# An attention loop with its steps reordered, its keys and queries split once per head pair, and a shorter weight conversion

## The chip, the cores and the metric

The kernel runs on one core of a Trainium2 chip. The metric is the device time of one execution in microseconds. Engines are named as the profile names them: PE (matrix multiply), PEld (its weight loads), DVE (vector), ACT (scalar), POOL (GpSimd) and SP (the queue from which nearly all DMAs of the attention stage are issued).

## What is computed

Attention over 4 batches and 8 heads, with queries averaged in pairs, then a switch layer with 8 experts, then a product layer. Cut to what matters:

```python
q_pool = q.reshape(B, H, S // 2, 2, D).mean(axis=3)      # B, H, S, D = 4, 8, 1152, 64
scores = np.matmul(q_pool, k.transpose(0, 1, 3, 2)) / np.sqrt(D)
attn = softmax(scores)
x = np.matmul(attn, v)                                   # 2304 tokens of 512
# tokens with x @ w_skip > 0 go through one expert: relu(xc @ w1[e]) @ w2[e]
# then h = (x @ m1) * (x @ m2); out = (h @ w3) @ w_out
```

Everything is held to float32 accuracy, so an operand is split into a rounded high part and a low remainder where the matmul runs in the faster `float32r` format.

## The kernel before

The attention stage walks 16 head pairs (4 batches times 4 pairs), nine steps a pair, 144 steps in one loop (L707). A step handles one tile of 128 queries of one head, or (the fifth of a pair, `TILES[l] is None`) the last 64 queries of both heads. In step `i` the program issues, for three different tiles at once:

- `emit_t(i-2)` and `emit_c`: nine 128 x 128 transposes of the exponentials of two steps earlier (L275), and their copies out of PSUM in three groups, by ACT, DVE and ACT (L294);
- `emit_e(i-1)`: the exponential of the step before, on ACT (L264), which needs the maximum;
- `emit_s(i)`: the score matmuls (L241), six of 384 columns, nine in the fifth step, into the same three PSUM banks that the transposes of this step used, each bank once its copy is done; then `emit_x(i)`, the row maximum on DVE (L252);
- two calls of `emit_pv`: each is one block of value matmuls (L311), two float32 matmuls of 64 weight columns, which the profile shows as four. A pair has 18 blocks, nine for its first 320 queries and nine for the other 256. This text calls such a block a value unit.

The order on PE is: value unit, transposes, value unit, scores. Each engine works through its own instructions in the order of the program. `tc.manual_schedule()` keeps the written order; waits between engines are semaphores that the framework sets from the data.

**Preparation.** While pair `p` runs, `prep(p+1, j)` at steps 1 to 6 makes the next pair's operands on POOL. The scores are exact because `KS[i][h]` holds the high part of a head's keys in partitions 0 to 63 and the low part in 64 to 127, and `QS[i][h][0]` holds the high part of the queries twice. So `load` fetches every head's keys and queries twice, into both halves of the partitions (eight DMAs of 64 partitions a pair), `prep_k` copies 128 partitions (L181) and subtracts in the upper 64 (L182), `prep_s` adds the two query halves and scales (L193, L194), `prep_q` splits (L203, L204) and fills `BD` (L206, 64 partitions). `ld_kh` copies the high keys of both heads into `KH` by two DMAs. All of it is done per head, with two buffers `i = p % 2`.

**Conversion.** Four weight matrices arrive as float64 and are turned into float32 in 40 chunks of 128 x 512 by `conv_ops`: three DVE operations on integers (L90, L93, L95) assemble the float's bits, POOL squares the high word (L91), and a fourth DVE operation (L97) sets tiny values to zero by that square. The result is stored by SP. `side` advances the conversion by two of its four parts a step (each `yield` ends a part) where no routing is under way.

**Routing.** After each batch of four pairs `route_ops` computes the expert of each token, in parts that `side` hands out; among them are POOL's ten indirect DMAs (L397, L410), which scatter token numbers, and five groups of output transposes (L430). In batches 0 to 2 these stand inside the loop: the scatters are issued in step 1 of pairs 6, 10 and 14, ahead of `prep(p+1, 0)`.

After the loop come the expert tiles and the output layer, from about 612 us on.

Of the kernel before, what the change touches and what calls it, by code (L numbers as in the profile page):

```python
# [43 lines left out]
def body(ctx, tc, q, k, v, w9, w1, w2, m1, m2, w3t, wo, cst, mcst, ids, out, dbg=None):  # L44
# [29 lines left out]
    def conv_ops(erl):  # L74
        def ld(name, c):
            h = erl.tile([128, CW, 2], I32, tag="ch", name="ch", bufs=3)
            SP.dma_start(h, wsrc[name].rearrange("(p n) t -> p n t", p=128)[:, c * CW:(c + 1) * CW, :])
            return h
        nxt = [ld(*conv_q[0]), ld(*conv_q[1])]
        yield  # L80
        st = None
        for n, (name, c) in enumerate(conv_q):
# [4 lines left out]
            m = erl.tile([128, CW], F32, tag="cm", name="cm", bufs=2)  # L87
            o = erl.tile([128, CW], F32, tag="co", name="co", bufs=2)
# [13 lines left out]
        SP.dma_start(*st)  # L102
# [13 lines left out]
    if True:  # L116
# [7 lines left out]
        KH = mid.tile([128, S], F32R, name="kh")  # L124
# [8 lines left out]
        def load(p, h):  # L133
            if p >= NP:
                return
            b, hp = divmod(p, NHP)
            r = slice(64 * h, 64 * h + 64)
            qr = erl.tile([128, 2, SQ], F32, tag="qr", name="qr", bufs=3)
            kr = erl.tile([128, S], F32, tag="kr", name="kr", bufs=3)
# [4 lines left out]
            rawq[p, h], rawk[p, h] = qr, kr  # L144

        def load_first():
            r = [slice(64 * h, 64 * h + 64) for h in range(2)]
            for h in range(2):
                rawq[0, h] = erl.tile([128, 2, SQ], F32, tag="qr", name="qr", bufs=3)
# [18 lines left out]
        def load_v(p):  # L168
# [3 lines left out]
            vr = mid.tile([128, 2, KT, HD], F32, tag="vr", name="vr", bufs=3)  # L172
# [14 lines left out]
        def prep_s(p, h, fast, c0=0, c1=SQ):  # L187
            qr = rawq[p, h]
            if c0 == 0:
                pre[p, h] = erl.tile([128, SQ], F32, tag="qsum", name="qsum", bufs=2)  # L190
# [19 lines left out]
        def ld_kh(p):  # L210
            if p < NP:
                for h in range(2):
                    SP.dma_start(f(KH[64 * h:64 * h + 64]), f(KS[p % 2][h][0:64]))

        def prep(p, j):
            if p >= NP:
                return
            h, u = divmod(j, 3)
            if u == 0:
                prep_k(p, h, 0, S, False)  # L220
            elif u == 1:
                prep_s(p, h, False)
            else:
                prep_q(p, h, False)
# [5 lines left out]
        def emit_s(i, c, evac):  # L230
# [4 lines left out]
            if t is None:  # L235
                seq = [(qs[h][0][:, 512:640], ks[h]) for h in range(2)] + [(BD[p % 2], KH)]
# [206 lines left out]
        def side(kinds):  # L443
# [239 lines left out]
        with tc.manual_schedule():  # L683
# [18 lines left out]
            ld_kh(0)  # L702
            for h in range(2):
                load(1, h)
            load_v(1)
            SP.dma_start(tab.rearrange("(p n) o -> p (n o)", p=128), padt)
            for i in range(NSTEP + 7):  # L707
# [8 lines left out]
                if l in (4, 7):  # L716
                    load(p + 2, l // 7)
                if l == 0 and p >= 1:
# [5 lines left out]
                for n in (2 * i - 14, 2 * i - 13):  # L724
# [7 lines left out]
                if pvs[0]:  # L732
                    emit_pv(*pvs[0])
# [9 lines left out]
                if pvs[1]:  # L743
# [214 lines left out]
```

## Time and profile before

| what | us |
|---|---|
| median of three runs | 1169.83 |
| lowest and highest run | 1162.92, 1172.56 |
| span of the profiled execution | 1168.7 |
| of that, attention stage | 0 to 612 |

The page and the rows below come from one profiled execution; the record gives its span, from the first instruction to the last, and no separate total for it. All stretches of time are counted from the start of that span. A busy PE is not PE at its peak, since matmuls are pipelined and their ends are modelled; so the distance between the starts of two runs of matmuls is used here, not their busy time. In the timeline equal instructions in a row stand on one line with their count, and a bracket gives the idle time before and what ended it.

### The profile page before, as it was taken

The numbers are of one execution on the slowest core, as the hardware profiler recorded it, in microseconds if no ns is written. First come the engines' busy times: TensorE is split into PE (matmuls) and PEld (weight loads), VectorE is DVE, ScalarE is ACT, GpSimd is POOL, SyncE is SP. The second block draws the span as 40 slices with busy tenths as digits, with TensorE's granted clock in tenths as the row PEclk, the third lists the DMA queues.
The fourth block names the chain that finished last, engine by engine and source line by source line (L and its number), as shares of the span: only waits on it lengthen the run. The fifth ranks groups of instructions, "written<-read, shape, count | busy, mean of one in ns | idle before, by whom it ended". The sixth has DMA issues, their size and how long they took to land. (4 is left out here: it accounts for less than half of the span.)

```text
span 1168.7 us, 16655 instructions
## 1 busy us (share of the span) xinstructions
PE 1079.3 (92%) x6060; PEld 817.8 (70%) x6060; DVE 630.2 (54%) x880; ACT 474.9 (41%) x900; POOL 516.6 (44%) x473
## 2 busy tenths in 40 slices
PE   5999999997989978999999769999699999999995
PEld 4665665664556645656667658878498989999894
DVE  6699997666986659975653342425651212112120
ACT  3655554553546535555563042324442212212120
POOL 4975666049772378661693361445712020101100
PEclk9999998998999999999999979999899999999998
DMA  9867766367665287543351883243301010101000
GB/s 217 235 189 203 211 173 162 81 106 188 199 174 154 23 195 217 163 117 82 72 153 37 143 273 112 64 164 119 122 28 47 8 55 1 55 19 38 27 1 28
DMA packets 63881, 136.04 MB, mean 116 GB/s; under 512 B 13216, under 2 KB 22944, under 8 KB 63778
## 3 DMA queue, kind: packets, MB, share of 16 engines
q1 hardware_dynamic: 54578, 118.94, 38.8%
q0 software_dynamic: 6080, 14.26, 3.8%
q10 hardware_dynamic: 3120, 1.57, 0.7%
q8 instruction: 52, 0.85, 0.3%
q14 instruction: 51, 0.42, 0.1%
HBM read 103.93 MB, written 22.96 MB: 109 GB/s over the span
## 5 line engine op out<-in xcount | busy, mean ns | idle before, releaser
L252 DVE TENSOR_REDUCE sm<-s 128x1 f32<-128x1152 f32 x144 | 195.0, 1354 | 106.1 <-PE s L241 99.9
L241 PE MATMUL s<-k,q 128*128 128x384 f32 x864 | 208.2, 367 | 47.4 <-DVE pt L294 34.4
L241 PEld LDWEIGHTS s<-k,q 128*128 128x128 f32 x864 | 147.6, 193 | 117.3 <-ACT pt L294 46.3
L294 ACT COPY pt<-s 128x384 f32<-128x384 f32 x288 | 137.8, 479 | 211.6 <-PE s L275 210.3
L311 PE MATMUL vb<-pt,vr 128*64 128x256 f32 (+1 forms) x1152 | 204.8, 438 | 0.0
L275 PEld LDWEIGHTS s<-cs,p 128*128 128x128 f32 x1296 | 145.3, 145 | 68.4 <-issue 53.8
L264 ACT ACTIVATE p<-s,sm 128x1152 f32<-128x1152 f32 x144 | 177.0, 1229 | 38.9 <-DVE sm L252 38.9
L275 PE MATMUL s<-cs,p 128*128 128x128 f32 x1296 | 180.0, 286 | 2.0 <-ACT p L264 2.0
L883 POOL DMA_INDIRECT out_dram<-ar,ord x18 | 17.9, 993 | 272.8 <-ACT ar L882 268.1
L868 DVE TENSOR_TENSOR ar<-b,ar 128x384 f32<-128x384 f32 x48 | 26.8, 558 | 193.6 <-PE b L864 193.6
L311 PEld LDWEIGHTS vb<-pt,vr 128*64 128x64 f32 x1152 | 58.8, 137 | 60.6 <-issue 57.1
L182 POOL TENSOR_TENSOR k<-kr,k 64x1152 fp32r<-64x1152 f32 x31 | 83.4, 2689 | 33.8 <-DMA perm<-idt,sp 31.4
L294 DVE COPY pt<-s 128x384 f32<-128x384 f32 x144 | 79.5, 552 | 15.1 <-PE s L275 12.1
L869 ACT CAST CVh<-ar 128x384 fp32r<-128x384 f32 x48 | 24.7, 514 | 108.5 <-DVE ar L868 108.5
L397 POOL DMA_INDIRECT tab<-idt,si x20 | 19.9, 993 | 108.6 <-DVE sp L407 102.6
L91 POOL TENSOR_TENSOR cm<-ch 128x512 f32<-128x512 f32 x40 | 43.1, 1079 | 53.4 <-DVE co L97 36.7
L93 DVE SCALAR_TENSOR_TENSOR ca<-ch,ca 128x512 int32<-128x512 int32 x40 | 61.9, 1547 | 1.1
L497 PE MATMUL b<-W2h,CVh 128*128 128x512 f32 x176 | 60.7, 405 | 0.2
L497 PE MATMUL b<-W1h,CVh 128*128 128x512 f32 x176 | 60.1, 402 | 0.8 <-issue 0.7
L497 PE MATMUL b<-WPh,CVh 128*128 128x512 f32 x144 | 57.5, 399 | 0.0
L497 PE MATMUL b<-WPl,CVh 128*128 128x512 f32 x144 | 56.9, 395 | 0.0
L497 PE MATMUL b<-WPh,CVl 128*128 128x512 f32 x144 | 56.8, 395 | 0.0
(189 smaller groups left out, 1880.3 us busy)
## 6 DMA issues: line engine op xcount, KB each, us to landing
kr<-in_k_dram SPq DMA_DIRECT2D x62, 288.0 KB, 6.5
qr<-in_q_dram SPq DMA_DIRECT2D x60, 288.0 KB, 5.7
R<-in_w_dram SPq DMA_DIRECT2D x16, 1024.0 KB, 5.4
vr<-in_v_dram SPq DMA_DIRECT2D x16, 576.0 KB, 8.1
kh<-k SPq DMA_DIRECT2D x32, 288.0 KB, 4.7
ch<-in_w3t_dram SPq DMA_DIRECT2D x16, 512.0 KB, 4.1
ch<-in_m_dram SPq DMA_DIRECT2D x16, 512.0 KB, 4.2
x_d<-xr SPq DMA_DIRECT2D x16, 258.0 KB, 14.1
```

Source lines behind the costliest of these rows:

```text
L91: POOL.tensor_tensor(m, hf, hf, op=ALU.mult)
L93: DVE.scalar_tensor_tensor(a, h[:, :, 1], -0x40000000, a, op0=ALU.bitwise_and, op1=ALU.bitwise_or)
L182: (DVE if fast else POOL).tensor_tensor(ks[64:128, c0:c1], kr[64:128, c0:c1], f(ks[64:128, c0:c1]), op=ALU.subtract)
L241: m = PE.matmul(sp[:, c, 0:384], lhsT=lt, rhs=kk[:, 384 * c:384 * c + 384], start=(n == 0), stop=(n == len(seq) - 1))
L252: DVE.tensor_reduce(sm, sp[:, :, 0:384], axis=AX.XY, op=ALU.max, negate=True)
L264: ACT.activation(pt, sp[:, :, 0:384], AF.Exp, bias=sm, scale=1.0, accum_out=SM[b][:, hp, c:c + 1])
L275: m = PE.transpose(tp[:, u * 128:u * 128 + 128], src[:, kt * 128:kt * 128 + 128], ident)
L294: m = (DVE.tensor_copy(o, i_) if eng is DVE else ACT.copy(o, i_)).ins
L311: PE.matmul(acc[64 * h:64 * h + 64, 0:n], lhsT=vr[:, h, kt, :], rhs=pt[:, kt, h, :], start=(kt == 0), stop=(kt == KT - 1))
L497: PE.matmul(o, lhsT=lh[a], rhs=rh[b_], start=(first and n == 0), stop=(last and n == len(order) - 1))
L868: DVE.tensor_tensor(cv, pb[:, 0:GT], av, op=ALU.mult)
L869: ACT.copy(CV[0][:, c], cv)
```

## The change

The value units of a step move behind the exponential and stand together, ahead of the scores; they are issued half a step earlier in the loop's count. `load` fetches each pair's keys and queries once, in 128 partitions; POOL splits them once for both heads, in four preparation steps, and DMAs on SP stack the halves into `KS` and `QS`. `KH` is now where the split writes and has two buffers, so `ld_kh` remains for the first pair only. In the conversion the last DVE operation goes; POOL compares the square and multiplies (`mask`), one chunk later. The first two DVE operations now stand in one part, so a chunk has two parts, and `side` advances one part a step. Buffers of `qr`, `vr` and `qsum` drop from 3, 3, 2 to 2, 2, 1, those of `cm` rise to 3; the values are loaded at step 7.

```diff
+        def mask(name, c, a, m):
+            POOL.tensor_scalar(m, m, TINY * TINY, 1.0, op0=ALU.is_ge, op1=ALU.mult)
+            POOL.tensor_tensor(m, a.bitcast(F32), m, op=ALU.mult)
+            SP.dma_start(wd[name].rearrange("(p n) -> p n", p=128)[:, c * CW:(c + 1) * CW], m)
...
             DVE.tensor_scalar(a, h[:, :, 1], 0x07FFFFFF, 3, op0=ALU.bitwise_and, op1=ALU.logical_shift_left)
+            DVE.scalar_tensor_tensor(a, h[:, :, 1], -0x40000000, a, op0=ALU.bitwise_and, op1=ALU.bitwise_or)
             POOL.tensor_tensor(m, hf, hf, op=ALU.mult)
-            yield
-            DVE.scalar_tensor_tensor(a, h[:, :, 1], -0x40000000, a, op0=ALU.bitwise_and, op1=ALU.bitwise_or)
+            if st:
+                mask(*st)
+            st = (name, c, a, m)
             yield
             DVE.scalar_tensor_tensor(a, h[:, :, 0], 29, a, op0=ALU.logical_shift_right, op1=ALU.bitwise_or)
             yield
-            DVE.scalar_tensor_tensor(o, m, TINY * TINY, a.bitcast(F32), op0=ALU.is_ge, op1=ALU.mult)
-            if st:
-                SP.dma_start(*st)
-            st = (wd[name].rearrange("(p n) -> p n", p=128)[:, c * CW:(c + 1) * CW], o)
-            yield
...
-        def load(p, h):
+        def load(p):
...
-            for u in range(2):
-                SP.dma_start(qr[64 * u:64 * u + 64], q[b, hp, r])
-            for u in range(2):
-                SP.dma_start(kr[64 * u:64 * u + 64], k[b, hp, r])
+            SP.dma_start(rawk[p], k[b, hp])
+            SP.dma_start(rawq[p], q[b, hp])
...
         def prep(p, j):
...
+            if j == 0:
+                for c in range(3):
+                    cc = slice(384 * c, 384 * c + 384)
+                    POOL.tensor_scalar(kh[:, cc], rawk[p][:, cc], 1.0, 0.0, op0=ALU.mult, op1=ALU.add)
+                    POOL.tensor_tensor(KL[:, cc], rawk[p][:, cc], f(kh[:, cc]), op=ALU.subtract)
+                del rawk[p]
+            elif j == 1:
+                qr = rawq.pop(p)
+                s = pre[p] = erl.tile([128, SQ], F32, tag="qsum", name="qsum", bufs=1)
+                POOL.tensor_tensor(s, qr[:, 0], qr[:, 1], op=ALU.add)
+                POOL.tensor_scalar(s, s, 0.0625, 0.0, op0=ALU.mult, op1=ALU.add)
+            elif j == 2:
+                for h in range(2):
+                    r = slice(64 * h, 64 * h + 64)
+                    SP.dma_start(f(KS[i][h][0:64]), f(kh[r]))
+                    SP.dma_start(f(KS[i][h][64:128]), f(KL[r]))
+                s = pre.pop(p)
+                POOL.tensor_scalar(QN[0], s, 1.0, 0.0, op0=ALU.mult, op1=ALU.add)
+                POOL.tensor_tensor(QN[1], s, f(QN[0]), op=ALU.subtract)
+                for h in range(2):
+                    r = slice(64 * h, 64 * h + 64)
+                    POOL.tensor_scalar(BD[i][r, r], f(QN[1][r, 512:576]), 1.0, 0.0, op0=ALU.mult, op1=ALU.add)
             else:
-                prep_q(p, h, False)
+                for h in range(2):
+                    r = slice(64 * h, 64 * h + 64)
+                    for u in range(2):
+                        d = slice(64 * u, 64 * u + 64)
+                        if h == 0:
+                            SP.dma_start(f(QS[i][h][0][d, 0:576]), f(QN[0][r]))
+                        else:
+                            SP.dma_start(f(QS[i][h][0][d, 0:512]), f(QN[0][r, 0:512]))
+                            SP.dma_start(f(QS[i][h][0][d, 576:640]), f(QN[0][r, 512:576]))
+                        SP.dma_start(f(QS[i][h][1][d]), f(QN[1][r]))
...
-                if k is None:
-                    next(conv, None)
...
-                if l in (4, 7):
-                    load(p + 2, l // 7)
-                if l == 0 and p >= 1:
+                if l == 4:
+                    load(p + 2)
+                if l == 7 and p >= 1:
                     load_v(p + 1)
...
-                for n in (2 * i - 14, 2 * i - 13):
+                for n in (2 * i - 13, 2 * i - 12):
...
-                if pvs[0]:
-                    emit_pv(*pvs[0])
...
-                if pvs[1]:
-                    emit_pv(*pvs[1])
+                for u in pvs:
+                    if u:
+                        emit_pv(*u)
...
-                if ss and l == 6:
-                    ld_kh(p + 1)
-                if ss and 1 <= l <= 6:
+                if ss and 1 <= l <= 4:
                     prep(p + 1, l - 1)
```

## Rows read from the trace of the kernel before

**Rows 1.** Busy us of PE, PEld, DVE, ACT, POOL by stretch; clock, DMA share, GB/s

```profile
60.00:180.00 120.00, 115.16 (x712) 73.61 (x713) 113.64 (x123) 69.42 (x132) 80.08 (x72) 1.00 0.72 198
41.00:612.00 571.00, 534.66 (x3295) 345.39 (x3296) 439.36 (x553) 309.18 (x596) 350.50 (x317) 0.97 0.60 153
612.00:1168.70 556.70, 516.15 (x2633) 450.98 (x2633) 166.35 (x290) 146.32 (x271) 141.26 (x126) 0.97 0.24 70
```

**Rows 2.** Timeline of one clean step: start us, us, engine, line, operation [idle before]

```profile
588.43 1.32 PE L241 MATMUL s<-k,q 128*128 128x384 f32 x6
...
589.68 0.65 PE L311 MATMUL vb<-pt,vr 128*64 128x256 f32 x4
...
589.84 1.36 DVE L252 TENSOR_REDUCE sm<-s 128x1 f32<-128x1152 f32 x1 [1.66 <-PE s L241]
...
590.26 1.20 PE L275 MATMUL s<-cs,p 128*128 128x128 f32 x9
...
591.18 0.56 DVE L294 COPY pt<-s 128x384 f32<-128x384 f32 x1
...
591.40 0.65 PE L311 MATMUL vb<-pt,vr 128*64 128x256 f32 x4
...
591.88 1.23 ACT L264 ACTIVATE p<-s,sm 128x1152 f32<-128x1152 f32 x1
```

**Rows 3.** Score matmuls (L241) by stretch, one head pair each: PE, PEld, clock, DMA

```profile
76.60:111.30 34.70, 12.74 (x60) 9.52 (x58) 1.00 0.69 184
258.40:309.50 51.10, 14.59 (x58) 9.59 (x58) 0.90 0.75 204
418.80:468.10 49.30, 14.50 (x60) 9.87 (x58) 0.93 0.76 205
```

**Rows 4.** Timeline around the scatters of the second batch, POOL, DVE and PE

```profile
391.37 1.01 POOL L397 DMA_INDIRECT tab<-idt,si  x1 [34.03 <-DVE sp L407]
...
404.56 1.15 POOL L181 TENSOR_SCALAR k<-kr 128x1152 fp32r<-128x1152 f32 x1
...
416.43 2.65 POOL L182 TENSOR_TENSOR k<-kr,k 64x1152 fp32r<-64x1152 f32 x1 [10.72 <-DMA perm<-idt,sp]
...
431.44 1.09 DVE L97 SCALAR_TENSOR_TENSOR co<-cm,ca 128x512 f32<-128x512 f32 x1 [9.31 <-POOL cm L91]
...
434.98 1.65 PE L241 MATMUL s<-k,q 128*128 128x384 f32 x4 [6.39 <-DVE pt L294]
```

**Rows 5.** Timeline, DVE and POOL, at one preparation step

```profile
109.88 2.90 POOL L182 TENSOR_TENSOR k<-kr,k 64x1152 fp32r<-64x1152 f32 x1
...
110.31 3.03 DVE L93 SCALAR_TENSOR_TENSOR ca<-ch,ca 128x512 int32<-128x512 int32 x1
```

**Rows 6.** Groups of instructions, 41 to 612 us: count, busy us, mean ns, idle before

```profile
L97 DVE SCALAR_TENSOR_TENSOR co<-cm,ca 128x512 f32<-128x512 f32 x40 | 35.2, 879 | 22.3 <-POOL cm L91 19.3
...
L182 POOL TENSOR_TENSOR k<-kr,k 64x1152 fp32r<-64x1152 f32 x28 | 75.4, 2694 | 33.5 <-DMA perm<-idt,sp 31.4
...
L204 POOL TENSOR_TENSOR q<-qsum,q 128x512 fp32r<-128x512 f32 (+2 forms) x44 | 46.4, 1055 | 3.7
L193 POOL TENSOR_TENSOR qsum<-qr 128x576 f32<-128x576 f32 x28 | 45.1, 1610 | 1.6
L91 POOL TENSOR_TENSOR cm<-ch 128x512 f32<-128x512 f32 x40 | 43.1, 1079 | 53.4 <-DVE co L97 36.7 <-issue 11.1 <-DMA qr<-in_q_dram 4.2
```

**Rows 7.** Timeline of PE where runs stand beside other neighbours

```profile
564.85 1.32 PE L241 MATMUL s<-k,q 128*128 128x384 f32 x6
566.00 0.60 PE L430 MATMUL vb<-cs,ar 128*128 128x128 f32 x4
...
570.08 0.76 PE L311 MATMUL vb<-pt,vr 128*64 128x320 f32 x4
...
613.73 1.30 PE L311 MATMUL vb<-pt,vr 128*64 128x320 f32 x8
```

**Rows 8.** DMA issues: count, KB each, median us to landing

```profile
kh<-k SPq DMA_DIRECT2D x32, 288.0 KB, 4.7
```

More of the change, by code (lines that the diff above doesn't have):

```diff
@@ L123, in body @@
         BD = [mid.tile([128, 128], F32R, name=f"bd{i}") for i in range(2)]
-        KH = mid.tile([128, S], F32R, name="kh")
+        KH = [pl[i].tile([128, S], F32R, name=f"kh{i}") for i in range(2)]
+        KL = mid.tile([128, S], F32R, name="kl")
+        QN = [mid.tile([128, SQ], F32R, name=f"qn{x}") for x in "hl"]
         KS = [[pl[i].tile([128, S], F32R, name=f"k{h}{i}") for h in range(2)] for i in range(2)]
@@ L136, in load @@
             b, hp = divmod(p, NHP)
[L137 to L144 removed]
+            rawq[p] = erl.tile([128, 2, SQ], F32, tag="qr", name="qr", bufs=2)
+            rawk[p] = erl.tile([128, S], F32, tag="kr", name="kr", bufs=3)
+            SP.dma_start(rawk[p], k[b, hp])
+            SP.dma_start(rawq[p], q[b, hp])
         def load_first():
@@ L148, in load_first @@
             for h in range(2):
-                rawq[0, h] = erl.tile([128, 2, SQ], F32, tag="qr", name="qr", bufs=3)
+                rawq[0, h] = erl.tile([128, 2, SQ], F32, tag="qr", name="qr", bufs=2)
                 rawk[0, h] = erl.tile([128, S], F32, tag="kr", name="kr", bufs=3)
@@ L171, in load_v @@
             b, hp = divmod(p, NHP)
-            vr = mid.tile([128, 2, KT, HD], F32, tag="vr", name="vr", bufs=3)
+            vr = mid.tile([128, 2, KT, HD], F32, tag="vr", name="vr", bufs=2)
             SP.dma_start(vr, v[b, 2 * hp:2 * hp + 2].rearrange("h (p t) d -> p h t d", p=128))
@@ L189, in prep_s @@
             if c0 == 0:
-                pre[p, h] = erl.tile([128, SQ], F32, tag="qsum", name="qsum", bufs=2)
+                pre[p, h] = erl.tile([128, SQ], F32, tag="qsum", name="qsum", bufs=1)
             s = pre[p, h][:, c0:c1]
@@ L208, in prep_q, with ld_kh @@
                 del pre[p, h]
[L210 to L213, printed above, removed]
+        def ld_kh():
+            for h in range(2):
+                SP.dma_start(f(KH[0][64 * h:64 * h + 64]), f(KS[0][h][0:64]))
         def prep(p, j):
@@ L217, in prep @@
                 return
[L218 to L222, printed above, removed]
-            else:
-                prep_q(p, h, False)
+            i = p % 2
+            kh = KH[i]
+            if j == 0:
[20 more added lines that the diff above has]
+                    POOL.tensor_scalar(BD[i][r, r], f(QN[1][r, 512:576]), 1.0, 0.0, op0=ALU.mult, op1=ALU.add)
+            else:
+                for h in range(2):
+                    r = slice(64 * h, 64 * h + 64)
[7 more added lines that the diff above has]
+                        SP.dma_start(f(QS[i][h][1][d]), f(QN[1][r]))
         NSTEP = NP * NT9
@@ L235, in emit_s @@
             if t is None:
-                seq = [(qs[h][0][:, 512:640], ks[h]) for h in range(2)] + [(BD[p % 2], KH)]
+                seq = [(qs[h][0][:, 512:640], ks[h]) for h in range(2)] + [(BD[p % 2], KH[p % 2])]
             else:
@@ L701, in body @@
             prep_k(0, 1, 0, S, False)
-            ld_kh(0)
-            for h in range(2):
-                load(1, h)
+            ld_kh()
             load_v(1)
             SP.dma_start(tab.rearrange("(p n) o -> p (n o)", p=128), padt)
+            load(1)
             for i in range(NSTEP + 7):
```

5 lines of the change are left out of this document (2 added, 3 removed).

## The prediction

> **What bounds the kernel now.** I read the busy time by stage first. The attention stage (41 to 612 us) keeps PE busy for 534.7 of 571.0 us; after 612 us the program is the expert and output stage, which the change does not touch, so its 556.7 us are taken as they are [rows 1]. Inside attention I then read one clean step line by line [rows 2]: a score run starts at 588.43, the first value unit at 589.68, nine transposes at 590.26, the second value unit at 591.40. With the second unit as long as the first, the step is 1.25 + 0.58 + 1.14 + 0.58 = 3.55 us and PE never stops in it, so PE's own order sets its length. Steps whose value unit is 320 columns wide are 0.2 us longer, the ninth step of a pair has three more score matmuls (0.5 us); a pair of nine clean steps comes to 4 × 3.76 + 3.65 + 3 × 3.55 + 4.07 = 33.4 us, sixteen pairs to 534.6. The stage ends at 612, so 77 us are lost. 7.6 go to the start (the first pair takes 41 us) and about 16 to the routing matmuls of three batches, which PE must do anyway. The other 53 are stalls, and the pair windows show them [rows 3]: pair 2 takes 34.7 us, pairs 7 and 11 take 51.1 and 49.3. With 2.5 us of output transposes in each, these two lose 15 and 13, together 28; the remaining 25 are spread over the pairs in which weight conversion runs.
>
> Two causes stand behind the stalls. In pairs 7 and 11 POOL issues ten scatters of 1.0 us from 391.37 on and then sits until 416.43 for them to land; DVE, in order, waits 9.31 us for POOL's square (L91) before its last conversion step, and PE 6.39 us behind DVE's copy [rows 4]. In the conversion pairs DVE is busy 113.6 of 120 us [rows 1], and its conversion operations are long because they meet POOL: an L93 of 3.03 us at 110.31 stands beside a POOL subtraction of 2.90 us that began at 109.88 [rows 5], while L97, which seldom meets one, averages 0.88 [rows 6].
>
> **The change part by part.** *Order of the step.* Before, PE changes four times a step between 128-column and 64-column weights: scores, value unit, transposes, value unit, scores. After, it is scores, transposes, two value units, scores: two changes. What one change costs: two value units of 320 columns in a row last 1.30 us where one lasts 0.76 [rows 7], so the second adds 0.54; a separate one takes 0.58 plus the 0.11 by which 0.76 exceeds the narrow unit's 0.65 [rows 2], 0.69. The difference is 0.15. The other end: scores followed directly by 128-column transposes take 1.15 (564.85 to 566.00) instead of 1.25 [rows 7], and the transposes then start without the slower first one, which I put at 0.05. Sum 0.30 a step. Bounds: 0.25 if the transposes gain nothing, 0.33 if they gain 0.08. 137 steps have scores or transposes beside value units, so 137 × 0.30 = 41 us.
>
> What takes the place of the value unit ahead of the transposes? They need the exponential of two steps earlier. Counted from the start of the transposes of one step: the maximum starts 0.27 after it (the last score matmul drains, then 0.1), takes 1.36, the exponential 1.23 after that [rows 2], and about 0.15 passes until PE may go: 3.0 us. The new step is 3.55 - 0.30 = 3.25. So the wait is hidden by 0.2 us in a narrow step and 0.4 in a wide one; before it was hidden by 0.6. The scores' wait for DVE's copy keeps 0.3. This is the cover that the sum needs, and any DVE work that delays the maximum by more than that now reaches PE. Queued behind a late maximum are the exponential on ACT and the evacuation copy on DVE.
>
> *Conversion.* DVE loses L97: 35.2 us of busy time [rows 6], 0.88 a chunk. It still does one step with two operations, then one step with one, instead of two and two. POOL gains a comparison and a product per chunk: the product like L91, 1.08 [rows 6]; the comparison, one input and 512 columns, between 0.5 (half of L91) and 1.1; I take 0.6. 40 × 1.7 = 68 us on POOL, which has the room (350 of 571 busy). New is a wait: the buffer that DVE's first operation writes is free only when POOL's product of two chunks earlier has read it. Outside the scatters POOL runs less than two steps late, so it costs nothing there; if that cover goes, the maximum and the copy stand behind it.
>
> *Preparation.* Two-input POOL work per pair was 2 × 2.69 + 2 × 1.61 + 3 × 1.06 = 11.8 us; split once per pair in 128 partitions it is three pieces of 384 (0.81 each at L91's rate), one L193 and one of 576 (1.2): 5.2 [rows 6]. With the two products of each chunk (4.5 chunks a pair, 9.7 against 4.9) the two-input total goes from 16.7 to 14.9, and no piece is longer than 1.6. So DVE meets POOL about as often and for a shorter time. But a late maximum costs more now, since the cover has shrunk. I set the 25 us of spread stalls unchanged. Bounds: they vanish (-25) or double (+25).
>
> *DMAs.* Per pair eight half-partition loads and two copies of KH (ten of 288 KB) become two full loads of 576 KB, four stacking copies of 288 KB and ten of Q (eight of 144 KB and more): 2.9 MB become 3.5. SP issues 26 instead of 20 a pair at about 0.5 us, 13 of 33 us. A KH copy, the same kind of transfer, lands in 4.7 us [rows 8], and DMA is busy 72% in the conversion pairs [rows 1]. POOL has Q ready about four steps ahead of the next pair, the ten issues take 5 us, landing 5 more: 10 against 13 us. I cost it at nothing; the cover is 3 us, and what would be late is the next pair's first score run.
>
> [...]
>
> *Scatters.* The change leaves the scatters and puts less behind them. Only POOL's 64-partition subtraction waited for their landing, not the 128-partition copy before it at 404.56 [rows 4]. After, the first POOL operation on fewer than 128 partitions is the copy into BD, at the end of the preparation. So K and Q are split at once after issue (13 us + about 9 = 22 us after 391.37), the BD copy waits to 25, then a square and the delayed product: done 28.5 after the first scatter. DVE stands at its new wait for that product from about 17.5 on, does its operations, maximum and copy, and PE goes on at about 31.5 where it would at 21.4: 10 us lost in each of pairs 7 and 11, by which time Q has landed. 28 become 20: 8 us gained. Bounds: 0 and 28.
>
> *The rest.* Second buffers, a later value load, one step's shift of the value units and one buffer for the query sum are set at 0 ± 3, hidden behind the same PE work.
>
> **Sum.** 1168.7 - 41 - 8 = 1119.7 against the profile's span. The median of the runs shown is 1169.8, 1.1 above the span, so I predict **1121 us**.
>
> **Rivals.** *Conversion swallows it.* [...] For it: the 3.03 us of rows 5 and the thin cover; against it: shorter POOL pieces. The 80 conversion steps keep their old length, only the other 57 gain: 57 × 0.30 + 8 = 25, so 1145. [...]
>
> *Everything opens.* The spread stalls go too, since DVE has 35 us less to do: 41 + 8 + 20 = 69, so 1101. Against it: DVE is 95% busy there.
>
> *The transposes wait for the exponential every step*, so the reorder gains nothing and only the scatter term is left: 1162. Against it: 3.0 against 3.25.
>
> *Slower: stacked keys and queries land late.* Place: first score run of each pair; path: POOL split, SP behind the conversion's store (which waits for POOL), ten issues, landing behind the loads of the pair after. It decides from a stall of 49 / 15 = 3.3 us a pair on: at twice the 10 us that I count, 20 against 13, it is 7 a pair, 105 - 49 = 56 slower: 1226. For it: DMA already 72% busy; against: stacking starts four steps ahead.
>
> *The change doesn't do what it says*: the value units, though issued together, could still be spaced 0.58 apart; the pair of units at 613.73 excludes that [rows 7].
>
> **How the numbers follow.** Forecast 0.55 (its own range 1105 to 1135), conversion swallows it 0.20, everything opens 0.10, exponential 0.07, late stacking 0.08. A measurement of this kernel tells about 1% from no change, 12 us. Faster: 0.55 + 0.20 + 0.10 = 0.85; same: 0.07; slower: 0.08. The range runs from 1097 (41 + 8 + 24 taken off) to 1157 (conversion pairs lose a further 12 by the doubled stalls); it leaves out the last two cases and the far ends.
>
> **What would show it.** Right: a narrow clean step of about 3.25 us; scores to transposes 1.15; one run of eight value matmuls of about 1.1 us a step; L97 gone and L93 shorter; pairs 7 and 11 near 40 us, with DVE's first conversion operation ended by POOL's product. Wrong: PE idle before transposes, released by the exponential; PE idle before the first score run of a pair, released by a DMA into q or k; DVE's conversion operations as long as before; pairs 7 and 11 still near 50.

## The result, and the profile after

The changed kernel takes 1135.28 us (median of 4 runs, 1134.05 to 1137.0) beside 1169.01 for the kernel before (4 runs, the three shown ahead of the prediction and one more): a ratio of 0.9711, 95% interval 0.9676 to 0.9747. It is faster by 33.7 us, inside the range on record, where 48 were forecast. The profiled execution took 1137.0 us, its span 1135.1. (Line numbers moved: scores are L267 after, L241 before; transposes L301, values L337, conversion L94, L95, L101, POOL's square L96, its comparison L80 and product L81.)

The first view sets the stages beside [rows 1]; columns as there.

```profile
60.00:180.00 120.00, 111.71 (x729) 81.64 (x726) 96.49 (x113) 72.34 (x136) 97.24 (x81) 0.97 0.66 195
41.00:581.00 540.00, 498.72 (x3318) 367.43 (x3317) 380.04 (x515) 316.32 (x598) 356.29 (x328) 0.97 0.63 177
581.00:1135.00 554.00, 515.19 (x2632) 450.94 (x2630) 166.65 (x290) 146.21 (x271) 145.40 (x131) 0.97 0.24 71
```

The last stage keeps its 554 us (556.7 before). Attention ends at 581 instead of 612, and in the conversion pairs (60 to 180 us) DVE is busy 96.5 us of 120 instead of 113.6, POOL 97.2 instead of 80.1. One clean step, narrow value units, the timeline that answers to [rows 2]:

```profile
56.89 1.23 ACT L290 ACTIVATE p<-s,sm 128x1152 f32<-128x1152 f32 x1
...
57.34 1.34 PE L267 MATMUL s<-k,q 128*128 128x384 f32 x6
...
58.52 1.14 PE L301 MATMUL s<-cs,p 128*128 128x128 f32 x9
...
59.59 1.08 PE L337 MATMUL vb<-pt,vr 128*64 128x256 f32 x8
...
60.60 0.62 PE L267 MATMUL s<-k,q 128*128 128x384 f32 x2
```

From the scores at 57.34 to those at 60.60 the step takes 3.26 us, where it took 3.55. Scores to transposes take 1.18, and eight value matmuls stand together for 1.08. The exponential that the transposes need began at 56.89 and ends at 58.12, 0.4 us before them. But not all pairs are clean. Score matmuls by stretch, pairs 4, 6, 10 and 15 (clock ahead of the last two columns):

```profile
139.50:182.10 42.60, 13.96 (x60) 9.71 (x58) 0.92 0.76 216
215.90:261.00 45.10, 13.46 (x60) 9.99 (x58) 0.89 0.50 137
371.20:417.10 45.90, 13.45 (x59) 10.00 (x58) 0.85 0.52 142
549.30:581.10 31.80, 12.63 (x60) 9.67 (x58) 1.00 0.67 197
```

Pair 15 takes 31.8 (34.3 before). Pairs 6 and 10 (45.1 and 45.9 us) now hold the long stalls that pairs 7 and 11 held in [rows 3], and pair 4 (like pair 8) has a stall that was not there before; the granted clock falls to 0.85 to 0.92 in them. The groups that answer to [rows 6], and the waits (us in total, times, longest):

```profile
L95 DVE SCALAR_TENSOR_TENSOR ca<-ch,ca 128x512 int32<-128x512 int32 x40 | 45.1, 1127 | 1.4
L101 DVE SCALAR_TENSOR_TENSOR ca<-ch,ca 128x512 int32<-128x512 int32 x40 | 36.5, 913 | 0.0
L94 DVE TENSOR_SCALAR ca<-ch 128x512 int32<-128x512 int32 x40 | 31.7, 793 | 43.4 <-POOL cm L81 33.6 <-DMA ch<-in_m_dram 4.9 <-DMA ch<-in_w3t_dram 4.9
...
L80 POOL TENSOR_SCALAR cm<-cm 128x512 f32<-128x512 f32 x40 | 80.1, 2002 | 2.7
L81 POOL TENSOR_TENSOR cm<-ca,cm 128x512 f32<-128x512 f32 x40 | 51.4, 1285 | 19.3 <-DVE ca L101 16.2
...
L222 POOL TENSOR_TENSOR kl<-kr,kh 128x384 fp32r<-128x384 f32 x40 | 42.3, 1057 | 3.3
```

```profile
PE s L267 <- DVE pt L320: 38.2, 13, 9.8
...
SPq L82 <- POOL cm L81: 116.4, 24, 10.2
```

The comparison (L80) takes 2.00 us, not 0.6. With the product (1.29) it puts 131.5 us on POOL. A piece of the key split (L222) takes 1.06 where 0.81 was priced. DVE waits 33.6 us for that product at L94, PE waits 38.2 us behind DVE, and SP, in order, stands 116.4 us at the stores of the product (L82), with loads of weights and stacking copies behind it. It also goes the other way round. In pair 4 POOL's product was done at 134.8, but SP issued its store only at 142.92, behind ten stacking copies of queries that began at 133.86; POOL's square three chunks on needs that buffer and stands 8.16 us for the store to land:

```profile
147.41 1.35 POOL L96 TENSOR_TENSOR cm<-ch 128x512 f32<-128x512 f32 x1 [8.16 <-DMA w3t<-cm]
```

So what makes POOL late in pair 4 is in part this wait, and not only its work. At the scatters (the place of [rows 4], one batch earlier):

```profile
235.21 0.97 POOL L436 DMA_INDIRECT perm<-idt,sp  x1 [0.30 <-issue]
236.25 0.51 POOL L221 TENSOR_SCALAR kh<-kr 128x384 fp32r<-128x384 f32 x1
...
249.67 1.26 POOL L81 TENSOR_TENSOR cm<-ca,cm 128x512 f32<-128x512 f32 x1
...
250.97 1.25 DVE L94 TENSOR_SCALAR ca<-ch 128x512 int32<-128x512 int32 x1 [10.07 <-POOL cm L81]
...
255.01 1.65 PE L267 MATMUL s<-k,q 128*128 128x384 f32 x4 [9.79 <-DVE pt L320]
```

POOL no longer waits for the scatters to land: 0.07 us after the last one it splits the keys. The product is done only at 250.9, DVE has stood 10.07 us at its new wait, and PE 9.79.

### The profile page after: what moved, and what is told of

The parts are those of the page before. It is cut to its first block, busy times and chain, and to the rows that moved or that the text cites. A ratio compares the mean times of both kernels' runs of the same rounds, so it can differ in the third digit from the quotient of the medians.

```text
span 1135.1 us, 16867 instructions
## 1 busy us (share of the span) xinstructions
PE 1038.1 (91%) x6060; PEld 836.9 (74%) x6060; DVE 566.8 (50%) x840; ACT 479.9 (42%) x900; POOL 525.3 (46%) x493
## 3 DMA queue, kind: packets, MB, share of 16 engines
q1 hardware_dynamic: 63698, 127.79, 39.5%
## 5 line engine op out<-in xcount | busy, mean ns | idle before, releaser
L267 PE MATMUL s<-k,q 128*128 128x384 f32 x864 | 207.1, 366 | 54.2 <-DVE pt L320 40.4
L267 PEld LDWEIGHTS s<-k,q 128*128 128x128 f32 x864 | 147.6, 193 | 125.4 <-DVE pt L320 46.4
L337 PE MATMUL vb<-pt,vr 128*64 128x256 f32 (+1 forms) x1152 | 174.6, 425 | 2.4 <-DVE lw L375 1.9
L301 PE MATMUL s<-cs,p 128*128 128x128 f32 x1296 | 173.5, 281 | 2.1 <-ACT p L290 2.1
L301 PEld LDWEIGHTS s<-cs,p 128*128 128x128 f32 x1296 | 154.1, 145 | 13.5 <-ACT p L290 7.0
L337 PEld LDWEIGHTS vb<-pt,vr 128*64 128x64 f32 x1152 | 71.2, 138 | 57.4 <-issue 25.7
L80 POOL TENSOR_SCALAR cm<-cm 128x512 f32<-128x512 f32 x40 | 80.1, 2002 | 2.7
L96 POOL TENSOR_TENSOR cm<-ch 128x512 f32<-128x512 f32 x40 | 44.9, 1122 | 40.1 <-DMA w3t<-cm 27.2
L81 POOL TENSOR_TENSOR cm<-ca,cm 128x512 f32<-128x512 f32 x40 | 51.4, 1285 | 19.3 <-DVE ca L101 16.2
```

The costliest lines, as they stand in the source:

```text
L80: POOL.tensor_scalar(m, m, TINY * TINY, 1.0, op0=ALU.is_ge, op1=ALU.mult)
L81: POOL.tensor_tensor(m, a.bitcast(F32), m, op=ALU.mult)
L267: m = PE.matmul(sp[:, c, 0:384], lhsT=lt, rhs=kk[:, 384 * c:384 * c + 384], start=(n == 0), stop=(n == len(seq) - 1))
L301: m = PE.transpose(tp[:, u * 128:u * 128 + 128], src[:, kt * 128:kt * 128 + 128], ident)
L337: PE.matmul(acc[64 * h:64 * h + 64, 0:n], lhsT=vr[:, h, kt, :], rhs=pt[:, kt, h, :], start=(kt == 0), stop=(kt == KT - 1))
```

## The experiments

Medians are of five runs each (four for the changed kernel), ratios against runs of the kernel before on the same chip, whose median lay between 1169 and 1175; so kernels of different rows are compared by ratio. This table says where in attention each kernel spends its time. It is worked out from the traces: the us from one pair's last score matmul to the next pair's, added over pairs (pairs 2, 3, 4, 8, 12 carry conversion; 6, 7, 10, 11 lie around scatters and carry conversion too). The new conversion also changes its pace: while routing is under way a step advances half a chunk where it advanced a quarter, so that in the changed kernel pairs 6 and 10 hold nine of DVE's integer operations instead of five, and pair 12 holds none. No run changes this pace alone.

```
kernel         median   ratio (95%)             pair 0  pair 1  2,3,4,8,12  6,7,10,11  5,9,13-15
before         ~1170    1                       41.0    35.6    183.9       171.0      180.1
reorder_only   1161.38  0.9901 (0.9870-0.9931)  40.2    34.4    185.3       179.3      172.2
prep_only      1125.64  0.9590 (0.9539-0.9640)  45.6    33.4    169.6       144.4      176.2
split3         1157.11  0.9895 (0.9862-0.9928)  41.1    33.9    180.3       159.5      179.8
order_undone   1151.66  0.9822 (0.9792-0.9852)  44.9    33.4    178.7       161.6      175.3
old_conv       1104.75  0.9410 (0.9379-0.9442)  45.5    30.9    162.6       142.4      165.8
after          1135.28  0.9711 (0.9676-0.9747)  44.9    30.9    180.2       159.3      165.9
plain_mask     1117.44  0.9515 (0.9483-0.9547)  44.8    30.9    167.2       152.2      166.7
ca4            1135.28  0.9672 (0.9620-0.9724)  45.2    30.9    173.7       156.5      168.3
plain_ca4      1118.72  0.9517 (0.9464-0.9571)  45.4    30.9    172.3       147.7      167.3
ca4_late       1111.93  0.9516 (0.9483-0.9548)  45.1    30.9    158.7       148.1      174.8
plain_late     1103.34  0.9402 (0.9365-0.9440)  45.1    30.9    157.7       147.6      166.9
best1          1091.17  0.9298 (0.9248-0.9349)  40.8    30.9    166.4       133.1      166.0
best2          1119.27  0.9580 (0.9546-0.9614)  40.5    30.9    157.0       146.3      188.6
```

### One part alone

**reorder_only**, the order of the step in the kernel before:

```diff
-for n in (2 * i - 14, 2 * i - 13):
+for n in (2 * i - 13, 2 * i - 12):
...
-                if pvs[0]:
-                    emit_pv(*pvs[0])
...
-                if pvs[1]:
-                    emit_pv(*pvs[1])
+                for u in pvs:
+                    if u:
+                        emit_pv(*u)
```

> The kernel before with the order of the step alone: both value units of a step stand together, behind the transposes, half a step earlier in the sequence; conversion, preparation and DMAs are those of before. Theory (a step is 0.28 to 0.30 shorter, wherever it stands): 137 steps give 38 to 41 us, 1128 to 1131. Rival (the thinner cover of the exponential gives it back in the conversion steps): only 57 steps gain, 16 us, about 1153.

Measured 1161.38, a gain of 11: neither. The profiled execution was the slowest of the five (1166.83), and in it attention ends where it did before (the columns add up to 611.4 and 611.6); so its rows show where the order gains and loses, not the 11. Pairs 5, 9 and 13 to 15 gain 7.9, pair 1 1.2; the conversion pairs lose 1.4, and the pairs around the scatters lose 8.3. DVE's last conversion operation and three moments of pair 7 show where:

```profile
L97 DVE SCALAR_TENSOR_TENSOR co<-cm,ca 128x512 f32<-128x512 f32 x40 | 36.5, 913 | 35.4 <-POOL cm L91 32.5
```

```profile
257.89 2.61 POOL L182 TENSOR_TENSOR k<-kr,k 64x1152 fp32r<-64x1152 f32 x1 [15.90 <-DMA perm<-idt,sp]
...
263.54 0.69 PE L241 MATMUL s<-k,q 128*128 128x384 f32 x1 [6.29 <-POOL q L203]
...
272.50 1.09 DVE L97 SCALAR_TENSOR_TENSOR co<-cm,ca 128x512 f32<-128x512 f32 x1 [15.30 <-POOL cm L91]
```

POOL waits 15.9 us for the scatters to land, and now the next pair's first score run, which comes sooner, waits 6.29 for POOL's queries (1.67 before); DVE's wait for the square (L97) is 32.5 us in all where it was 19.3. A shorter step comes sooner to the same late POOL.

**prep_only**, the new preparation with order and conversion of before (the changed kernel with these two undone):

> The kernel before with the new preparation alone (one split a pair, stacking copies, new loads and buffer numbers); order of the step and conversion as before. If the preparation takes away stalls whichever order runs: the kernel with new order and new preparation (1104.8) plus 137 steps of 0.28 us, 38, is 1143, some 30 under the kernel before. If it is worth only the scatter term that the prediction gave it: 8, about 1163. If the new preparation needs the new order: no change, 1172.

Measured 1125.64, 0.959 (0.9539 to 0.964): 48 us of 1170 (42 in attention by the table), more than any theory gave. The scatter group falls from 171.0 to 144.4, the conversion pairs from 183.9 to 169.6; only pair 0 loses 4.6. DVE's four conversion operations, and POOL behind its last scatter of that batch:

```profile
L96 DVE SCALAR_TENSOR_TENSOR cm<-cm,ca 128x512 f32<-128x512 f32 x40 | 36.8, 919 | 3.0
L94 DVE SCALAR_TENSOR_TENSOR ca<-ch,ca 128x512 int32<-128x512 int32 x40 | 32.4, 811 | 0.0
L92 DVE SCALAR_TENSOR_TENSOR ca<-ch,ca 128x512 int32<-128x512 int32 x40 | 31.2, 780 | 1.1
L89 DVE TENSOR_SCALAR ca<-ch 128x512 int32<-128x512 int32 x40 | 25.0, 626 | 0.0
```

```profile
235.72 0.98 POOL L434 DMA_INDIRECT perm<-idt,sp  x1 [0.30 <-issue]
236.77 0.51 POOL L219 TENSOR_SCALAR kh<-kr 128x384 fp32r<-128x384 f32 x1
...
246.40 0.58 POOL L237 TENSOR_SCALAR bd<-qnl 64x64 fp32r<-64x64 f32 x2
```

Of the kernel before, the same view had beside L97 of [rows 6]:

```profile
L93 DVE SCALAR_TENSOR_TENSOR ca<-ch,ca 128x512 int32<-128x512 int32 x40 | 61.9, 1547 | 1.1
```

With L90's 30.3 the four took 172.5 us there and take 125.4 here; the one that stood beside POOL's long subtraction in [rows 5], L93, falls from 1547 to 780 ns (L92). And POOL goes on at once after the scatters, where it stood 10.72 in [rows 4]: the only preparation on fewer than 128 partitions now comes at its end, at 246.40, and finds the scatters landed. Where the waits show POOL held by that landing, it works on 64 partitions (L182 before, 31.4 us in all, and in split3, 14.2; the copy into BD in best2, 5.8); why, no run shows.

**split3**, the kernel before with only its key split in pieces:

```diff
-                prep_k(p, h, 0, S, False)
+                for c in range(3):
+                    prep_k(p, h, 384 * c, 384 * c + 384, False)
```

> The kernel before, POOL's split of the keys (rounding and 64-partition subtraction) done in three pieces of 384 columns instead of one of 1152; nothing else. Theory L (the spread stalls come from single long POOL operations that hold up DVE's): the stalls outside the scatter pairs, 25 us, fall to under 10, those of the scatter pairs stay: 1152 to 1160. Theory A (they come from the amount of two-input work on POOL, which is the same here): 1168 to 1176.

```profile
L93 DVE SCALAR_TENSOR_TENSOR ca<-ch,ca 128x512 int32<-128x512 int32 x40 | 41.7, 1044 | 1.1
...
L182 POOL TENSOR_TENSOR k<-kr,k 64x384 fp32r<-64x384 f32 x84 | 95.3, 1134 | 28.9 <-DMA perm<-idt,sp 14.2 <-PE vb L431 7.9
```

1157.11 is the time of theory L, but not its place: the conversion pairs gain 3.6, the scatter group 11.5. DVE's L93 falls from 1547 to 1044 ns on average, though the two-input work is if anything more (95.3 us for L182 against 75.4 in [rows 6]). Outside the scatter group the pairs gain 10 us: the conversion pairs 3.6, pairs 1, 5, 9 and 13 6.6. The new preparation took 21 from the same pairs, 14.3 and 7.1. So shorter pieces explain part of L93's length and about half of what the preparation took from the spread stalls, nearly all of it in pairs 1, 5, 9 and 13; that the other half goes with the amount of work is not shown by a run of its own. Around the scatters pairs 7 and 11 fall from 51.1 and 49.2 to 38.2 and 40.1, while pairs 6, 10 and 14 rise from 35.3 to 41.4, 39.7 and 39.9, by stalls that are told under *What stays open*.

### Taking one part out of the changed kernel

**order_undone**, the old order of the step back in the changed kernel:

> The changed kernel with the old order of the step (one value unit ahead of the transposes, one behind), all else as changed. If the order is worth 39 us on its own and the rest of the change costs about 5: 1174. Rival (with the old, thicker cover the late mask no longer reaches PE, so the rest of the change is a gain): 1150 to 1160.

1151.66: the rival's time. Against the changed kernel (0.9822 against 0.9711) the order is worth 13 us of 1170 there.

**old_conv**, the old four-operation conversion back in the changed kernel, in place:

```diff
-        def mask(name, c, a, m):
-            POOL.tensor_scalar(m, m, TINY * TINY, 1.0, op0=ALU.is_ge, op1=ALU.mult)
-            POOL.tensor_tensor(m, a.bitcast(F32), m, op=ALU.mult)
...
+            DVE.scalar_tensor_tensor(m, m, TINY * TINY, a.bitcast(F32), op0=ALU.is_ge, op1=ALU.mult)
+            if st:
+                SP.dma_start(*st)
```

> The changed kernel with the old conversion: four DVE operations a chunk in the old two plus two schedule, POOL only squares. T1: the waits of DVE for POOL's product go with it, pairs 4 and 8 near 34 us, the scatter stalls shrink since DVE waits only for the square; against it stand 35 us more on DVE: 1112 to 1125. T2 (SP's queue): 1131 to 1140. A third theory, that the shorter conversion on DVE is what made the new order pay: over 1145.

1104.75, better than T1 had it: the new conversion costs the changed kernel 0.9711 - 0.941 = 0.0301, 35 us. Conversion pairs take 162.6 instead of 180.2, the scatter group 142.4 instead of 159.3. DVE has one operation more a chunk, and the kernel loses nothing by it. The operation that the change drops takes 34.0 us on DVE here. But the three others take 908, 848 and 648 ns on average here and 1127, 913 and 793 in the changed kernel, 17 us more in all, beside POOL's comparison and product: half of what the dropped operation saved on DVE came back.

**plain_mask**, the comparison replaced by a plain operation:

```diff
-POOL.tensor_scalar(m, m, TINY * TINY, 1.0, op0=ALU.is_ge, op1=ALU.mult)
+POOL.tensor_scalar(m, m, 0.0, 1.0, op0=ALU.mult, op1=ALU.add)
```

> The changed kernel with POOL's comparison replaced by a multiplication and an addition of the same 128x512 tile that gives 1 everywhere (the flush of tiny weights is left out). Theory T1 (the comparison of 1.93 us makes POOL late, DVE waits for its product at its new buffer wait, PE behind it): the instruction falls to about 0.6, POOL has 52 us less, the stalls of about 9 us in pairs 4 and 8 and the 1 to 2 us in others go, the two scatter stalls of 10 stay: 1112 to 1120. Rival T2 (SP's queue of stacking copies makes stores and loads of the weights late): 1131 to 1137, pairs 4 and 8 still about 42 us.

```profile
L80 POOL TENSOR_SCALAR cm<-cm 128x512 f32<-128x512 f32 x40 | 28.1, 702 | 0.0
```

0.70 us for the same tile in place of 2.00, and 1117.44: T1's time. The comparison is 0.0196 of the 0.0301, 23 us of 35. Pairs 4 and 8 still take 36.6 and 37.0, so some 12 us of the conversion's cost are not the comparison. These are of T2's kind, which the time alone does not tell: in pair 4 of this run POOL stands 11.30 us for a store of an earlier chunk to land (8.16 in the changed kernel).

### Why buffers did not help, and what did

**ca4**, four buffers for the integer word (two) and the mask (three):

> The changed kernel with four buffers instead of two for DVE's integer word and four instead of three for the mask (paid with one raw-key buffer, which stands empty). Theory W (DVE's wait for the buffer turns a late POOL into a late maximum): the two scatter stalls of 10 and those of pairs 4 and 8 shrink to what POOL is late on the whole, 1110 to 1122. Theory C (POOL and DVE only get in each other's way in SBUF, or POOL has too much work, so buffers are no help): 1130 to 1138.

```profile
SPq L82 <- POOL cm L81: 129.2, 23, 11.9
...
DVE ca L94 <- DMA ch<-in_m_dram: 19.1, 5, 8.5
DVE ca L94 <- DMA ch<-in_w3t_dram: 11.4, 3, 4.5
...
PE s L267 <- DMA q<-qnh: 11.4, 4, 4.9
PE s L267 <- DMA q<-qnl: 6.9, 4, 4.0
```

The median stays at 1135.28 (the ratio falls by 0.0039, and the intervals overlap): theory C by its time, but the waits tell another story than C. DVE's 33.6 us at L94 for POOL's product are gone; in their place it waits 30.5 for loads of weights at the same line, and PE 18.3 for the stacked queries. All of these are issued by SP, which stands 129.2 us at the stores.

**plain_ca4**, both edits:

> Both at once: no comparison (a multiplication and an addition that give 1 everywhere; the flush of tiny weights is left out) and four buffers for the integer word and the mask. Theory W: a POOL that is short of nothing and a wait that no longer reaches DVE leave neither the scatter stalls nor those of pairs 4 and 8: 1096 to 1104, at or under the kernel with the old conversion (1104.8). Theory C: the 1117 of the kernel without comparison stays, 1113 to 1118.

1118.72, nothing under plain_mask: buffers alone bring little with the comparison and nothing without it. Theory W fell: the buffer was the first thing DVE met, not the thing that was short.

**ca4_late**, ca4 with each store issued one chunk later:

```diff
-            if st:
-                mask(*st)
+            if so:
+                SP.dma_start(*so)
+            so = mask(*st) if st else None
```

> The changed kernel with four buffers each for the integer word and the mask, and the store of each finished chunk issued one chunk later on SP, so that SP seldom stands at a store whose product POOL has not done. With the buffers alone, DVE's 33.6 us of waiting for POOL's product became 30.5 us of waiting for loads of the weights and PE 18 us of waiting for stacked queries. Theory Q (SP, in order, stands at the store, and loads and stacking copies stand behind it): both shrink to a third, 1112 to 1122. Theory P (POOL has too much to do: 4.3 us a chunk, and each late chunk makes its own buffers late): 1128 to 1136.

```profile
SPq L98 <- POOL cm L81: 10.4, 8, 2.7
...
DVE ca L94 <- DMA ch<-in_w3t_dram: 2.8, 2, 2.6
...
DVE ca L94 <- POOL cm L81: 2.0, 1, 2.0
```

1111.93, at the lower end of theory Q's range, and 18 us under ca4 by ratio (17 in attention by the table): SP's wait for the product falls from 129.2 to 10.4, DVE's waits at L94 from 30.5 to 4.8, PE's for the queries to nothing. The conversion pairs take 158.7, less than with the old conversion (162.6), and that with the comparison still at 2.00 us. So the order of SP's queue carried these stalls. The late store was run only together with the four buffers, which give it room.

**plain_late**, the same without the comparison:

> The kernel with four buffers and the late store (1111.9), its comparison replaced by a multiplication and an addition that give 1 everywhere (the flush of tiny weights is left out). If the order of SP's queue was what four buffers alone could not mend, the late store takes as much from the kernel without comparison (1118.7) as it took from the one with it (1135.3 to 1111.9, 23), and no stall is left that the conversion makes: 1096 to 1102. If comparison and queue cost through the same stalls, so that either cure does for both: 1108 to 1112. The three stalls of 7 us inside the scatter series that the late store brought, which lie in pairs 6, 10 and 14 and end with no releaser that the profile shows, stay if they belong to the scatters' place in the sequence, and go if they came from POOL's being late.

```profile
PE s L269 <- DMA q<-qnh: 9.3, 2, 5.6
```

1103.34, between the two. By the table's rows the late store took 15 us here, and the comparison costs 9 beside it; by ratio it is 13 for each. The ratio, 0.9402, is that of the kernel with the old conversion (0.9410): of the conversion's 35 us nothing is left. Pairs 7 and 11 take 40.0 and 39.4, since their queries come late after the scatters. The three stalls went.

### Two attempts at a better kernel

**best1**, old_conv with a second query-sum buffer and the preparation one step earlier:

```diff
-                if ss and 1 <= l <= 4:
-                    prep(p + 1, l - 1)
+                if ss and l <= 3:
+                    prep(p + 1, l)
```

> New order, new preparation, old four-operation conversion; the query sum with two buffers again (paid with the empty raw-key buffer), and the preparation one step earlier in each pair. The second query-sum buffer should give back the 4 us of the third score step; the earlier preparation puts the split of the keys ahead of the scatters in POOL's order, so that the queries of the next pair are stacked earlier and the 5 and 2 us lost at the start of pairs 7 and 11 shrink: 1094 to 1100. If the stacking is late for another reason (SP's queue): 1099 to 1102.

Pair 7, score matmuls by stretch:

```profile
237.60:270.80 33.20, 13.25 (x58) 9.39 (x57) 1.00 1.01 299
```

1091.17, ratio 0.9298 (0.9248 to 0.9349): the fastest measured, under both kernels. Pair 7 takes 33.2 where old_conv takes 39.5, and pair 11 32.9 instead of 36.5, so the scatter group takes 133.1 instead of 142.4; pair 0 has its 4.7 us back. The conversion pairs take 3.8 more than in old_conv, which no run explains.

**best2**, the same cures for the new conversion, and a minimum in place of the comparison:

```diff
+POOL.tensor_scalar(m, m, 1.0 / (TINY * TINY), 1.0, op0=ALU.mult, op1=ALU.min)
```

> The changed kernel with four buffers for integer word and mask, the store one chunk late, the preparation one step earlier, the second query sum of the first pair in a tile that stands empty, and POOL's comparison replaced by a multiplication and a minimum with 1 (a weight between zero and the threshold would be scaled down instead of set to zero; zeros stay zero). If the minimum takes about 0.6 us as a multiplication and addition does, and neither SP nor the scatters hold up DVE: 1078 to 1088, under the best kernel so far, 1091.2. If the minimum costs 1.9 like the comparison: 1100 to 1112. If the product on POOL is enough to keep POOL late: 1092 to 1100.

```profile
L80 POOL TENSOR_SCALAR cm<-cm 128x512 f32<-128x512 f32 x40 | 82.2, 2055 | 0.0
```

```profile
171.43 0.43 DVE L94 TENSOR_SCALAR ca<-ch 128x512 int32<-128x512 int32 x1 [6.99 <-DMA ch<-in_w3t_dram]
```

The minimum costs 2.06, like the comparison, and 1119.27 is above all three ranges. Its conversion pairs are the shortest of all (157.0); pairs 5, 9 and 14 take 41.7, 39.8 and 41.9, where best1 has 33.6, 33.6 and 33.5. POOL's price alone does not explain these. In pair 5 DVE stands 6.99 us for a load of the weights (the second line) and PE 5.38 behind it; in pair 9 it is 6.03 and 4.41. The late store did not cure this. In pair 14 PE, DVE and ACT stop together, as told under *What stays open*.

## Why the prediction held, point by point

The time was in the range by three errors that nearly cancel: as a total it was luck, though steps of the working came out. In us of 1170, from the ratios, one part after the other: preparation 48 gained (8 forecast), order 21 gained on top of it (0.959 to 0.941; 41 forecast), conversion 35 lost (nothing forecast).

*Order of the step: the size of a clean step was right, the count of steps was not.* 0.30 a step was forecast; pairs 1 and 15 give 33.42 - 30.92 and 34.31 - 31.73 between prep_only and old_conv, 0.28 a step. "137 × 0.30" took every step as clean. Between the same two kernels pair 0 gains nothing, the conversion pairs 7.0 of some 12.5 us, and the pairs around the scatters 2.0 of some 10: where conversion or scatters make DVE or POOL late, the shorter step meets them sooner. The failed step is the sentence that any DVE work that delays the maximum by more than the thin cover "now reaches PE": it was written down and then not priced. What it takes depends on the rest: the order gave 11 alone (by the medians), 13 in the changed kernel, 21 with the new preparation and the old conversion.

*Preparation: "I set the 25 us of spread stalls unchanged" failed.* With the preparation alone the conversion pairs lose 14.3 us of stall and pairs 1, 5, 9, 13 a further 7.1 (from the pair times), some 21 of the 25. That is near one end of the forecast's bounds (-25 to +25). The forecast saw that the preparation's two-input work on POOL falls from 11.8 to 5.2 us a pair, counted the new products against it (16.7 to 14.9), and let the thinner cover cancel the rest. This run has the thick cover and no products, so it tests the preparation without them: DVE's conversion falls by 47 us. In the changed kernel, with the thin cover, little is left of the spread stalls either in pairs 1, 2 and 3 (30.9, 31.2 and 32.6 us); what it loses in pairs 4 and 8 is the conversion's. In the traces L93 falls from 1547 to 780 ns as the preparation's two-input work on POOL falls from 166.9 to 87.2 us; split3 shows that its piece length matters too (1044 ns). That the two-input work is what counts was the author's estimate: the one-input work of the key and query split falls as well, from 80.4 to 45.8 us, and no run tells the two apart or shows by what means one engine lengthens the other's operations. The *scatter term* failed with it: the wait for landing is gone, as forecast, but so is the whole loss of 28 when the conversion stays on DVE (pairs 7 and 11 fall from 51.1 and 49.2 to 35.6 and 36.4). The 10 us in each of two pairs that were forecast to remain did come (9.79 on PE in pair 6), by the forecast's own path: DVE stands at its new wait, and PE goes on 31.5 us after the first scatter (223.51), as worked out. They lie one pair earlier than forecast, in pairs 6 and 10, and they belong to the conversion, not to the preparation.

*Conversion: two terms.* For the comparison, "between 0.5 (half of L91) and 1.1; I take 0.6" failed: 2.00 measured, outside its own bounds. A plain multiplication and addition of the same shape takes 0.70, so the bounds were right for arithmetic and wrong for a comparison, which no row of the trace before showed. And "Outside the scatters POOL runs less than two steps late, so it costs nothing there" failed: with 4.4 us of POOL a chunk (1.12 + 2.00 + 1.29) instead of 2.8, POOL is late in pairs 4 and 8. What no term of the sum holds is the order on SP: the store now stands right behind the product, SP waits for it, and stacking copies and stores hold each other up. The queue is named ("SP behind the conversion's store") only in the fourth rival. The conversion's faster pace beside routing was not priced either, and no run tells its share.

*DMAs and stacking: nothing, as forecast, in this kernel.* PE waits 0.4 us for stacked queries, though in pair 4 the copies hold up a store and, through it, POOL by 8.16. The rival's path is real: PE waits 18.3 us on it in ca4 and 9.3 in plain_late, once DVE no longer stalls first. That its 3 us of cover are thin is shown; that it would make the kernel slower is not.

*The rest: 0 ± 3 was outside.* One buffer for the query sum costs 4 us at the start, in the changed kernel's trace:

```profile
18.61 0.42 DVE L192 TENSOR_TENSOR qsum<-qr 128x256 f32<-128x256 f32 x1 [6.80 <-POOL q L203]
...
20.79 0.66 PE L267 MATMUL s<-k,q 128*128 128x384 f32 x1 [5.40 <-DVE q L202]
```

DVE waits 6.80 for POOL to leave the single buffer, PE 5.40; best1 gave it back.

*Rivals.* "Conversion swallows it" (1145) had the right part: the conversion pairs take 180.2 us, little less than the 183.9 of before. Against the kernel before, two of DVE's three conversion operations got shorter (1547 to 1127 and 1129 to 913 ns, while the first went from 757 to 793), as in prep_only; against old_conv, which has the same preparation, all three got longer, by 17 us in all. But 23 of the 35 us ended with the comparison's length, and the rest with the late store and its buffers, so lateness of POOL and SP was the larger part. "Everything opens" (1101) is the time of the kernel once the old conversion is put back, 1104.75, with less from the order and more from the preparation than that rival had. The exponential held PE up in no clean step: none of PE's waits in the changed kernel's attention (41 to 581 us) is put down to it.

*What stays open.* ca4_late has three stalls of about 7 us inside the scatter series, in pairs 6, 10 and 14:

```profile
503.52 0.97 POOL L438 DMA_INDIRECT perm<-idt,sp  x1 [0.30 <-issue]
...
504.28 1.36 DVE L280 TENSOR_REDUCE sm<-s 128x1 f32<-128x1152 f32 x1 [6.65 <-remote]
...
506.40 0.86 ACT L322 COPY pt<-s 128x384 f32<-128x384 f32 x2 [6.93 <-remote]
...
506.93 1.01 PE L269 MATMUL s<-k,q 128*128 128x384 f32 x2 [5.19 <-ACT pt L322]
```

PE, DVE and ACT all stop while POOL scatters; the releaser is not on this core's record ("remote"), DVE goes on at about the end of the last scatter, ACT and PE two to three us later. split3 and best2 have such stalls, plain_late, best1 and the changed kernel do not. Pair 14 has no conversion, so the conversion's own waits don't explain it. The runs don't settle the cause. Also open are the share of the conversion's faster pace beside routing and the loads that come late in pairs 5 and 9 of best2.

## What to carry to other kernels

A right total can be made of wrong terms: run the parts alone before you believe the sum. A shorter step on the bounding engine is worth its full size only where no other engine is late, so take away lateness first (here the preparation, 48 us) and count the step afterwards. When work moves to another engine, look at every in-order queue that waits for its result: here SP stood 129.2 us at stores put right behind a late product (ca4), while DVE waited 30.5 for the loads and PE 18.3 for the copies that SP issues, and in pair 4 of the changed kernel a store in turn stood behind ten copies and held up POOL by 8.16. Here twice the buffers alone did not mend that; with them, issuing the store one chunk later did.

## What the runs showed of the hardware

- On POOL a 128x512 fp32 tensor_scalar took 0.70 us with multiply and add (plain_mask), 2.00 with a comparison (the changed kernel) and 2.06 with a minimum (best2): 2.9 times the time of the plain operation. No run shows why.
- A DVE operation on 128x512 words took 1547, 1044 or 780 ns on average with the same instruction, in three kernels that differ in the preparation beside it (before, split3, prep_only).
- After the stall of ca4_late that is shown under *What stays open* PE went on at a lower granted clock: behind the 5.19 us that it stood idle before 506.93, the clock (the column after the busy times) was 0.50 until 510.1, and 0.99 from there to 514.0:

```profile
506.70:510.10 3.40, 3.17 (x9) 2.67 (x10) 1.49 (x3) 1.77 (x4) 3.31 (x4) 0.50 0.46 125
510.10:514.00 3.90, 3.30 (x25) 2.23 (x23) 3.47 (x4) 2.17 (x4) 3.53 (x5) 0.99 0.98 84
```

Two score matmuls took 1.01 us there (506.93) and 0.62 in the changed kernel at 60.60. So the pair times with stalls hold a little more than the stalls; what this adds was not measured by itself.
